# Attention tails of two heads in one product with both heads' values side by side, and one more batch's outputs turned by DMA

## The chip, the cores and the metric

The kernel runs on one core of one Trainium2 chip. The metric is the device time of one execution in microseconds (us). The kernel before was run eight times; one more execution was recorded by the hardware profiler, and all rows below come from that one.

The engines are TensorE (PE in the profile, its weight loads PEld), VectorE (DVE), ScalarE (ACT), GpSimd (POOL) and SyncE (SP). SyncE and GpSimd issue the DMAs; "SPq" and "POOLq" are their queues.

## The reference

Inputs are q, k and v of 8 batches x 8 heads x 576 positions x 64 elements, a forget gate f of 8 x 8 x 576, and two weight matrices of 512 x 2048 and 2048 x 512. A forgetting attention comes first, then a feed-forward layer with a gated activation:

```python
scores = scale * q @ k.T                     # per batch and head, 576 x 576
cum = np.cumsum(np.log(np.clip(f, 1e-4, 1)), axis=-1)
scores = where(causal, -1e9, scores + cum[:, None] - cum[None, :])
attn = softmax(scores)
x = (attn @ v)  ->  rows = batch x position (4608), columns = head x 64 (512)
h = x @ w_in
out = (h * sigmoid(h)) @ w_out               # 4608 x 512, float32
```

## The kernel before

**Attention.** The decay is folded into the values: each value row is multiplied by exp(-cum) of its position (up to a constant), and a 65th column holds that factor itself, so that one product gives both the weighted sum and the divisor. The unnormalised weights are exp(scores), kept in bf16 with keys on the partitions.

The 576 positions of a batch are split in three: the first 128 ("heads", done for all batches ahead of the loop), the next 384 ("rest", three blocks of 128), and the last 64 ("tail"). The main loop works on units n = 0 to 31. A unit is one batch b = n // 4 and two heads; two units make a query pair m = n // 2, so m = 0 to 15 and a batch is two pairs. For a unit:

- SyncE loads q and k of both heads (`load_qk`, L158), once a batch the tails (L168) and the values (L179). GpSimd casts to bf16 (`cast_qk`, L400 and L404) and scales the values by their weights (L414). SyncE turns q and k by a DMA transpose into `qkT` (`transposes`, L428).
- `scores` (L460) multiplies keys and queries in three chunks on TensorE; ScalarE takes the exponent into `u` (L464) for the rest rows and into `ut` (L476) for the tail rows; VectorE masks the diagonal blocks (L469, L483).
- `attend` (L491) multiplies the weights by the values into a PSUM tile `dn`: 18 matmuls of 65 columns for the six rest blocks (L507: two heads x three blocks), and ten for the tails (L516). VectorE takes the reciprocal of the 65th columns (L524) and multiplies (L525) into the SBUF tile `xr`.
- `back` (L532) turns a pair's `xr` so that model columns lie on the partitions, as the feed-forward part needs them. Where `BY_DMA[m]` is true this is two DMA transposes on SyncE's queue (L539 for the rest, L543 for the tails); else seven transposes on TensorE into a PSUM tile `tx` (L549) and two VectorE copies (L552, L555).

**The tail product before.** `ut` of a unit holds, for each of five key blocks, 64 weight columns of head 0, 64 columns of zeros, and 64 columns of head 1. The five matmuls of head 0 take the first 128 columns (head 0 and zeros) against head 0's values; the five of head 1 take the last 128 (zeros and head 1) against head 1's values, and all ten add into the same 128 x 65 block, so that head 0's 64 rows land on partitions 0 to 63 and head 1's on 64 to 127. The zeros are written once by GpSimd (L735).

**Feed-forward.** `m1_chunk` computes 128 of the 2048 inner columns of one group of rows: four matmuls into a PSUM tile `hp` (L568), a tanh on ScalarE (L576), and a multiply on VectorE into `gt` (L577). `m2_part` adds four matmuls of 512 columns each into a PSUM tile `po` (L613); after four parts ScalarE copies it out (L623) and GpSimd issues the store (L592).

**Order.** The order on every engine is that of the program text. In the loop over m, attention steps alternate with slots: `slot(us)` adds feed-forward steps worth so many microseconds by a fixed count of columns, from the groups of rows that are in `ready`. A batch's rest group gets into `ready` one slot after its second pair's `back`, or two slots after it where that pair goes by DMA. One iteration reads: scores of unit n, slot, `back(m - 1)`, the remaining scores of n and the first of n + 1, slot, the remaining scores of n + 1, slot, `attend(n)`, `attend(n + 1)`, slot.

**PSUM.** Scores have two double-bank buffers of their own. `dn`, `tx`, `hp` and `po` share the pool `pbig` with the tag "big" and four buffers of one bank each; a new tile can be written when the last reader of the buffer's former tile is done.

The lines of the loop that set this order:

```python
        scores(n + 1, 1)
        scores(n + 1, 2)
        slot(piece, 2)
        attend(n)
        attend(n + 1)
        slot(min(3.5, max(0.8, behind() - LAG)) if m > 1 else 0.8, 1)
```

The functions that the change touches:

Of the kernel before, what the change touches and what calls it, by code (L numbers as in the profile page):

```python
# [9 lines left out]
ALU = mybir.AluOpType  # L10
FP32 = mybir.dt.float32
BF16 = mybir.dt.bfloat16
P = 128
# [5 lines left out]
def kernel(  # L19
# [10 lines left out]
    nc = tc.nc  # L30

    B, H, S, D = q.shape
# [6 lines left out]
    ST = S - SM  # L39
    NM = SM // P  # L40
    NR = NM - 1
# [4 lines left out]
    NQ = NU // 2  # L46
# [9 lines left out]
    const = ctx.enter_context(tc.tile_pool(name="const", bufs=1))  # L56
# [4 lines left out]
    recp = ctx.enter_context(tc.tile_pool(name="recp", bufs=2))  # L61
# [7 lines left out]
    pbig = ctx.enter_context(tc.tile_pool(name="pbig", bufs=4, space=bass.MemoryType.PSUM))  # L69
# [12 lines left out]
    kT0 = [const.tile([P, NP, P], BF16, name=f"kT0_{b}") for b in range(B)]  # L82
    v0 = [const.tile([P, H, D + 1], BF16, name=f"v0_{b}") for b in range(B)]
    vps = [const.tile([P, NM, H, D + 1], BF16, name=f"vp_{i}") for i in range(2)]
    uts = [const.tile([P, NM + 1, 3, ST], BF16, name=f"ut_{i}") for i in range(4)]
    vfs = [const.tile([P, H, D + 1], FP32, name=f"vf_{i}") for i in range(4)]


# [10 lines left out]
    def xg(g):  # L99
        if g not in xgs:  # L100
            tag, bufs = {4 * P: ("x4", 1), 2 * P: ("x2" if g < 3 else "xt", 2), RB: ("x3", 3)}[GW[g]]
            xgs[g] = xpool.tile([P, NCC, GW[g]], BF16, name=tag, tag=tag, bufs=bufs)
        return xgs[g]
# [45 lines left out]
    def head(p, i):  # L149
        return p // 2 * 4 + 2 * i + p % 2  # L150
# [69 lines left out]
    for i in range(2):  # L220
        for g in range(2):
            nc.vector.tensor_copy(
                out=sel[:, i, :].rearrange("p (u w r) -> p u w r", u=2, w=2)[:, g, :, :],
                in_=ident_bf[:, :].rearrange("p (r u i w) -> p u i w r", u=2, i=2, w=2)[
                    :, g, i, :, :
                ],
            )

    def keep_warm(n):
# [7 lines left out]
        out=f_sb[:, :], in0=f_sb[:, :], scalar1=1e-4, scalar2=1.0, op0=ALU.max, op1=ALU.min  # L237
# [207 lines left out]
    def scores(n, c):  # L445
        b, p = divmod(n, NP)
        if c == 0:
            us[n] = upool.tile([P, 2, UW], BF16, name="u", tag="u")
        u, ut = us[n], uts[n % 4]
        t = qkT[n]  # L450
        sc = psc.tile([P, 2, SM], FP32, name="sc", tag="sc")
        for kb, q0, q1, o in CHUNKS[c]:
            for i in range(2):
                r = slice(i * D, (i + 1) * D)
                if kb == 0:
                    kt = kT0[b][r, p, :]
                else:
                    k0 = RB if kb == NM else kb * P + RB
                    kt = t[r, k0 : k0 + P]
                nc.tensor.matmul(  # L460
                    sc[:, i, o : o + q1 - q0], lhsT=kt, rhs=t[r, q0:q1], start=True, stop=True
                )
        w = SM if c < 2 else T0
        nc.scalar.activation(  # L464
            out=u[:, :, c * SM : c * SM + w], in_=sc[:, :, 0:w], func=ACT.Exp, scale=scale
        )
        if c == 0:
            x = u[:, :, 0:RB].rearrange("p i (a t) -> p i a t", t=P)
            nc.vector.tensor_tensor(  # L469
                out=x,  # L470
                in0=x,
                in1=tri[:, None, None, :].to_broadcast([P, 2, NR, P]),
                op=ALU.mult,
            )
        if c == 2:
            nc.scalar.activation(  # L476
                out=ut[:, :, 0:3:2, :].rearrange("p k i t -> p i k t"),
                in_=sc[:, :, T0 : T0 + (NM + 1) * ST].rearrange("p i (k t) -> p i k t", t=ST),
                func=ACT.Exp,
                scale=scale,  # L480
            )
            x = ut[:, NM, 0:3:2, :]
            nc.vector.tensor_tensor(  # L483
                out=x, in0=x, in1=trit[:, None, :].to_broadcast([P, 2, ST]), op=ALU.mult
            )

    NGR = 2 * NR + 1

    BY_DMA = [2 * 2 <= m < NQ - 1 for m in range(NQ)]

    def attend(n):  # L491
        b, p = divmod(n, NP)
        if p % 2 == 0:
            xqs[n // 2] = xqp.tile([P, NGR, 2, D], BF16, name="xr", tag="xr", bufs=3)
        xq = xqs[n // 2]
        u, ut = us.pop(n), uts[n % 4]
        dn = pbig.tile([P, NGR, D + 1], FP32, name="dn", tag="big")

        def vals(kb, i):
            h = head(p, i)  # L500
            return v0[b][:, h, :] if kb == 0 else vbf[b][:, kb - 1, h, :]

        for i in range(2):
            for c in range(1, NM):
                for kb in range(c + 1):
                    o = AT[c, kb]
                    nc.tensor.matmul(  # L507
                        dn[:, i * NR + c - 1, :],
                        lhsT=u[:, i, o : o + P],
                        rhs=vals(kb, i),  # L510
                        start=(kb == 0),
                        stop=(kb == c),
                    )
        for i in range(2):
            for kb in range(NM + 1):
                nc.tensor.matmul(  # L516
                    dn[:, NGR - 1, :],
                    lhsT=ut[:, kb, i : i + 2, :].rearrange("p i t -> p (i t)"),
                    rhs=vals(kb, i),
                    start=(i == 0 and kb == 0),  # L520
                    stop=(i == 1 and kb == NM),
                )
        rec = recp.tile([P, NGR], FP32, name="rec", tag="rec")
        nc.vector.reciprocal(out=rec[:, :], in_=dn[:, :, D])  # L524
        nc.vector.tensor_tensor(  # L525
            out=xq[:, :, p % 2, :],
            in0=dn[:, :, 0:D],
            in1=rec[:, :, None].to_broadcast([P, NGR, D]),
            op=ALU.mult,
        )  # L530

    def back(m):  # L532
        b, c0 = m // 2, m % 2 * 2
        xq = xqs.pop(m)
        g, t0 = TAILS_OF[b]
        xr = xg(REST_OF[b])[:, c0 : c0 + 2, :]
        xt = xg(g)[:, c0 : c0 + 2, :].rearrange("p i t -> p (i t)")[:, t0 * P : (t0 + 1) * P]
        if BY_DMA[m]:
            nc.sync.dma_start_transpose(  # L539
                out=xr.rearrange("p i (a q) -> p (i a) q", q=P),  # L540
                in_=xq[:, 0 : 2 * NR, :, :].rearrange("p c w d -> p (c w d)"),
            )
            nc.sync.dma_start_transpose(  # L543
                out=xt[:, None, :], in_=xq[:, 2 * NR, :, :].rearrange("p w d -> p (w d)")
            )
            return
        tx = pbig.tile([P, NGR, P], BF16, name="tx", tag="big")
        for c in range(NGR):
            nc.tensor.transpose(  # L549
                tx[:, c, :], xq[:, c, :, :].rearrange("p w d -> p (w d)"), ident_bf[:, :]  # L550
            )
        nc.vector.tensor_copy(  # L552
            out=xr, in_=tx[:, 0 : 2 * NR, :].rearrange("p (i a) q -> p i (a q)", i=2)
        )
        nc.vector.tensor_copy(out=xt, in_=tx[:, 2 * NR, :])  # L555
# [115 lines left out]
    def behind():  # L671
        t = sum(4 * (GW[g] / 2.4 + 2.5) for g, _ in M1[at["m1"] :] if g in ready)
        t += sum(4 * (DM / 2.4 + 2.5) for g, _, _ in M2[at["m2"] :] if g in ready)
        return t / 1000
# [56 lines left out]
    ready.add(0)  # L731
    nc.gpsimd.memset(trit[0:ST, :], 0.0)
    make_upper_triangular(nc, trit[ST:P, :], val=1.0, diag=True)
    for t in uts:
        nc.gpsimd.memset(t[:, :, 1, :], 0.0)  # L735
    for t in vps:
        nc.gpsimd.memset(t[0:ST, NR, :, :], 0.0)
    load_w_out(0)
# [84 lines left out]
    def slot(us_, first=0):  # L823
        n = len(stores)
        fill(us_, first)
        store(n)
        for x in pending:
            x[0] -= 1
        while pending and pending[0][0] == 0:
            ready.update(pending.pop(0)[1])  # L830

    for m in range(NQ):
        n = 2 * m
        piece = 1.7 if m < 2 else 2.4
        scores(n, 0)
        scores(n, 1)
        prepare(n)
        slot(piece, 2)
        if m > 0:
            back(m - 1)  # L840
            if m % 2 == 0:
                b = m // 2 - 1
                pending.append([1 + BY_DMA[m - 1], [REST_OF[b]] + ([TAILS_OF[b][0]] if b == NM - 1 else [])])
        scores(n, 2)
        scores(n + 1, 0)
        prepare(n + 1)
# [3 lines that stand above are left out]
        slot(piece, 2)  # L850
        attend(n)
        attend(n + 1)
        slot(min(3.5, max(0.8, behind() - LAG)) if m > 1 else 0.8, 1)
    back(NQ - 1)
    ready.update([REST_OF[B - 1], TAILS_OF[B - 1][0]])
# [36 lines left out]
```

The softmax here doesn't subtract the row's maximum and nothing guards it: scores larger than these inputs give would overflow.

## Time and profile before

| | |
|---|---|
| time, median of 8 runs | 346.88 us (346.48 to 347.54) |
| profiled execution | 346.72 us, its span 344.9 us |
| TensorE busy | 334.5 us, 97% |
| ScalarE busy | 218.2 us, 63% |
| VectorE busy | 184.2 us, 53% |
| GpSimd busy | 130.0 us, 38% |
| granted TensorE clock | full speed throughout |

The span is what the engines' rows cover; 1.8 us of the execution lie outside it. A row of a timeline gives the start in us, the duration in us, the engine, the line, the operation, and how many were merged; a bracket at its end says how long the engine sat idle before it and what ended that. A group row gives the count, the busy time in us, the mean of one in ns, and the idle time before them. A wait row says who waited for whom: us in total, times, the longest. TensorE's matmuls are pipelined, so the duration of one (some 0.19 us at 65 columns) is longer than the spacing between two.

### The profile page before, as it was taken

Reading aid. Unit: us, or ns where it says so; the run is one execution under the profiler, and the core shown is the slowest. Engines: PE = TensorE matmul, PEld = TensorE weight load, DVE = VectorE, ACT = ScalarE, POOL = GpSimd, SP = SyncE. Lnnn points to the kernel's source line nnn. Section 1 sums busy time; section 2 is a strip of 40 time slices with the busy share of each in tenths; the row PEclk is TensorE's granted clock in tenths of the full one; section 3 lists DMA queues with packets and bytes.
Section 4 is the critical chain, followed back from the end, with each engine's and each line's share of the span. In section 5 each row is a group of like instructions: output and inputs, shape, how many; then the busy total and the mean of one; then the engine's idle time right before and its main releaser. Section 6 shows DMA issues by size and latency. Waiting matters only on the chain.

```text
span 344.9 us, 8892 instructions
## 1 busy us (share of the span) xinstructions
PE 334.5 (97%) x3567; PEld 199.1 (58%) x3567; DVE 184.2 (53%) x389; ACT 218.2 (63%) x401; POOL 130.0 (38%) x227
## 2 busy tenths in 40 slices
PE   7999999988998999999999999999999999999995
PEld 3654556656655556566565665656656565555664
DVE  4766645456567457367547653646645454535330
ACT  5866554786586866767759566595775934545341
POOL 8995234934527154155227128135420000010011
PEclk9999999999999999999999999999999999999999
DMA  8999999999688998798988899989932000010103
GB/s 157 201 185 219 196 166 151 240 210 187 165 187 186 199 196 170 173 200 178 162 205 159 163 171 218 158 181 193 155 86 55 34 32 30 32 53 29 42 37 87
DMA packets 141497, 50.44 MB, mean 146 GB/s; under 512 B 132368, under 2 KB 138768, under 8 KB 141456
## 3 DMA queue, kind: packets, MB, share of 16 engines
q1 hardware_dynamic: 131440, 32.70, 53.2%
q0 software_dynamic: 9856, 17.04, 20.9%
q8 instruction: 28, 0.46, 0.6%
q10 hardware_dynamic: 160, 0.13, 0.1%
q14 instruction: 13, 0.11, 0.1%
HBM read 36.85 MB, written 9.44 MB: 134 GB/s over the span
## 4 chain that ended last, share of the span: by engine, by line
PE 72%; DMA 14%; SPq 5%; POOL 4%; issue 2%; ACT 1%; DVE 1%; POOLq 0%
PE po L613 30%; PE hp L568 28%; PE sc L460 6%; PE dn L507 4%; DMA vf<-in_v_dram 4%; DMA w_out_bf<-in_moe_w_out_dram 3%; DMA qktf<-in_k_dram 3%; PE dn L516 2%; SPq L158 2%; SPq L428 2%; DMA qkb<-in_k_dram 1%; DMA qkT<-qkb 1%; SPq L168 1%; DMA kf<-in_k_dram 1%; POOL qkb L131 1%
## 5 line engine op out<-in xcount | busy, mean ns | idle before, releaser
L576 ACT ACTIVATE th<-hp 128x384 bf16<-128x384 f32 (+2 forms) x208 | 95.9, 476 | 90.3 <-PE hp L568 88.0
L577 DVE SCALAR_TENSOR_TENSOR gt<-th,hp 128x384 bf16<-128x384 bf16 (+2 forms) x208 | 105.9, 521 | 79.7 <-ACT th L576 76.3
L613 PE MATMUL po<-w_out_bf,gt 128*128 128x512 bf16 (+1 forms) x592 | 144.7, 374 | 0.0
L568 PE MATMUL hp<-x,w_in_bf 128*128 128x384 bf16 (+2 forms) x704 | 128.9, 321 | 0.2
L568 PEld LDWEIGHTS <-w_in_bf 128*128 128x128 bf16 x832 | 78.5, 98 | 55.2 <-issue 2.2
L613 PEld LDWEIGHTS <-gt 128*128 128x128 bf16 x592 | 54.6, 98 | 49.6 <-issue 2.1
L464 ACT ACTIVATE u<-sc 128x1024 bf16<-128x1024 f32 (+1 forms) x96 | 75.0, 821 | 12.3 <-PE sc L460 12.2
L592 POOL DMA_DIRECT2D out_dram<-osb x38 | 21.0, 554 | 131.5 <-ACT osb L623 89.2
L414 POOL TENSOR_TENSOR vp<-vf,w_bf 128x520 bf16<-128x520 f32 (+1 forms) x32 | 35.0, 1096 | 31.4 <-DMA vf<-in_v_dram 26.3
L469 DVE TENSOR_TENSOR u<-u,tri 128x768 bf16<-128x768 bf16 x32 | 22.7, 709 | 19.8 <-ACT u L464 19.8
L623 ACT ACTIVATE osb<-po 128x512 f32<-128x512 f32 (+1 forms) x37 | 22.0, 595 | 12.3 <-PE po L613 12.2
L483 DVE TENSOR_TENSOR ut<-ut,trit 128x128 bf16<-128x128 bf16 x32 | 10.9, 340 | 34.9 <-ACT ut L476 32.8
L400 POOL CAST qkb<-qf 128x384 bf16<-128x384 f32 x32 | 17.7, 552 | 31.4 <-DMA qf<-in_q_dram 27.9
L460 PE MATMUL sc<-qkT 64*128 64x128 bf16 (+1 forms) x640 | 26.5, 207 | 2.3 <-DMA qkT<-qkb 2.3
L460 PEld LDWEIGHTS <-qkT 64*128 64x128 bf16 x640 | 18.2, 94 | 13.4 <-issue 8.1
L476 ACT ACTIVATE ut<-sc 128x640 bf16<-128x640 f32 x32 | 23.3, 727 | 0.0
L507 PEld LDWEIGHTS <-u 128*128 128x128 bf16 x576 | 20.7, 98 | 3.7 <-issue 1.3
L507 PE MATMUL dn<-vp,u 128*128 128x65 bf16 x384 | 21.8, 193 | 0.0
L507 PE MATMUL dn<-v,u 128*128 128x65 bf16 x192 | 19.8, 193 | 1.1 <-DVE gt L577 1.1
L525 DVE TENSOR_TENSOR xr<-dn,rec 128x448 bf16<-128x448 f32 x32 | 20.0, 625 | 1.1
L400 POOL CAST qkb<-kf 128x384 bf16<-128x384 f32 x32 | 16.7, 522 | 7.5 <-DMA kf<-in_k_dram 7.5
L568 PE MATMUL hp<-xt,w_in_bf 128*128 128x256 bf16 x128 | 18.2, 272 | 0.3 <-DVE gt L577 0.2
(68 smaller groups left out, 203.6 us busy)
## 6 DMA issues: line engine op xcount, KB each, us to landing
out_dram<-osb POOLq DMA_DIRECT2D x32, 256.0 KB, 3.1
vf<-in_v_dram SPq DMA_DIRECT2D x26, 256.0 KB, 5.0
qf<-in_q_dram SPq DMA_DIRECT2D x64, 96.0 KB, 2.8
kf<-in_k_dram SPq DMA_DIRECT2D x64, 96.0 KB, 2.9
w_in_bf<-in_moe_w_in_dram POOLq DMA_DIRECT2D x4, 512.0 KB, 7.0
w_out_bf<-in_moe_w_out_dram POOLq DMA_DIRECT2D x4, 512.0 KB, 8.8
vf<-in_v_dram POOLq DMA_DIRECT2D x6, 256.0 KB, 10.2
qkb<-in_q_dram POOLq DMA_DIRECT2D x8, 128.0 KB, 5.1
```

What stands on the lines that cost most here:

```text
L400: nc.gpsimd.tensor_copy(out=t2[:, c0 : c0 + NR, :].rearrange("p c x -> p (c x)"), in_=t[:, :, :, :].rearrange("p c h d -> p (c h d)"),)
L414: nc.gpsimd.tensor_tensor(out=vbf[b][r, c, :, :], in0=vst[b][c][r, :, :], in1=w_bf[r, c + 1, b * H : (b + 1) * H, None].to_broadcast([n, H ...
L460: nc.tensor.matmul(sc[:, i, o : o + q1 - q0], lhsT=kt, rhs=t[r, q0:q1], start=True, stop=True)
L464: nc.scalar.activation(out=u[:, :, c * SM : c * SM + w], in_=sc[:, :, 0:w], func=ACT.Exp, scale=scale)
L469: nc.vector.tensor_tensor(out=x, in0=x, in1=tri[:, None, None, :].to_broadcast([P, 2, NR, P]), op=ALU.mult,)
L476: nc.scalar.activation(out=ut[:, :, 0:3:2, :].rearrange("p k i t -> p i k t"), in_=sc[:, :, T0 : T0 + (NM + 1) * ST].rearrange("p i (k t) ...
L507: nc.tensor.matmul(dn[:, i * NR + c - 1, :], lhsT=u[:, i, o : o + P], rhs=vals(kb, i), start=(kb == 0), stop=(kb == c),)
L568: nc.tensor.matmul(hp[:, :], lhsT=w_in_bf[:, cc, fc * P : (fc + 1) * P], rhs=xcols(g, cc), start=(cc == 0), stop=(cc == NCC - 1),)
L576: nc.scalar.activation(out=th[:, :], in_=hp[:, :], func=ACT.Tanh, scale=0.5)
L577: nc.vector.scalar_tensor_tensor(out=gt[:, fc, :], in0=th[:, :], scalar=1.0, in1=hp[:, :], op0=ALU.add, op1=ALU.mult,)
L613: nc.tensor.matmul(po[:, :], lhsT=gt[:, fc, tb * P : (tb + 1) * P], rhs=w_out_bf[:, fc, m0:m1], start=(fc == 0), stop=(fc == NFC - 1),)
L623: nc.scalar.activation(out=osb[:, :], in_=po[:, :], func=ACT.Copy, scale=0.5)
```

## The change

The tails leave `attend`, which keeps only the six rest blocks. A new function `attend_tails(m)` runs after both units of a pair: for each unit, five matmuls multiply the 128 weight columns of both heads by the values of both heads side by side (130 columns). The result holds four blocks of 64 x 65, of which two are used: head 0's rows with head 0's values, and head 1's rows with head 1's. VectorE takes one reciprocal for both units and then multiplies once for partitions 0 to 63 and once for 64 to 127. The zero columns of `ut` and the GpSimd writes of them go. `BY_DMA` becomes true for m = 2 and 3 too, so that batch 1's outputs are turned by DMA and its rest group gets ready one slot later.

```diff
-    uts = [const.tile([P, NM + 1, 3, ST], BF16, name=f"ut_{i}") for i in range(4)]
+    uts = [const.tile([P, NM + 1, 2, ST], BF16, name=f"ut_{i}") for i in range(4)]
...
-    BY_DMA = [2 * 2 <= m < NQ - 1 for m in range(NQ)]
+    BY_DMA = [2 <= m < NQ - 1 for m in range(NQ)]
...
-        dn = pbig.tile([P, NGR, D + 1], FP32, name="dn", tag="big")
+        dn = pbig.tile([P, 2 * NR, D + 1], FP32, name="dn", tag="big")
...
-        for i in range(2):
-            for kb in range(NM + 1):
-                nc.tensor.matmul(
-                    dn[:, NGR - 1, :],
-                    lhsT=ut[:, kb, i : i + 2, :].rearrange("p i t -> p (i t)"),
-                    rhs=vals(kb, i),
-                    start=(i == 0 and kb == 0),
-                    stop=(i == 1 and kb == NM),
-                )
...
+    def attend_tails(m):
+        b, h0 = m // 2, m % 2 * 4
+        xq = xqs[m]
+        dt = pbig.tile([P, 2, 2, D + 1], FP32, name="dt", tag="big")
+        for w in range(2):
+            ut = uts[(2 * m + w) % 4]
+            for kb in range(NM + 1):
+                vals = v0[b] if kb == 0 else vbf[b][:, kb - 1, :, :]
+                nc.tensor.matmul(
+                    dt[:, w, :, :],
+                    lhsT=ut[:, kb, :, :].rearrange("p i t -> p (i t)"),
+                    rhs=vals[:, h0 + w : h0 + 4 : 2, :],
+                    start=(kb == 0),
+                    stop=(kb == NM),
+                )
+        rec = recp.tile([P, 2, 2], FP32, name="rect", tag="rect")
+        nc.vector.reciprocal(out=rec[:, :, :], in_=dt[:, :, :, D])
+        for i in range(2):
+            r = slice(i * ST, (i + 1) * ST)
+            nc.vector.tensor_tensor(
+                out=xq[r, 2 * NR, :, :],
+                in0=dt[r, :, i, 0:D],
+                in1=rec[r, :, i, None].to_broadcast([ST, 2, D]),
+                op=ALU.mult,
+            )
...
-    for t in uts:
-        nc.gpsimd.memset(t[:, :, 1, :], 0.0)
...
         attend(n)
         attend(n + 1)
+        attend_tails(m)
```

More of the change, by code (lines that the diff above doesn't have):

```diff
@@ L476, in scores @@
             nc.scalar.activation(
-                out=ut[:, :, 0:3:2, :].rearrange("p k i t -> p i k t"),
+                out=ut[:, :, :, :].rearrange("p k i t -> p i k t"),
                 in_=sc[:, :, T0 : T0 + (NM + 1) * ST].rearrange("p i (k t) -> p i k t", t=ST),
@@ L481, in scores @@
             )
-            x = ut[:, NM, 0:3:2, :]
+            x = ut[:, NM, :, :]
             nc.vector.tensor_tensor(
@@ L495, in attend @@
         xq = xqs[n // 2]
-        u, ut = us.pop(n), uts[n % 4]
-        dn = pbig.tile([P, NGR, D + 1], FP32, name="dn", tag="big")
+        u = us.pop(n)
+        dn = pbig.tile([P, 2 * NR, D + 1], FP32, name="dn", tag="big")
         def vals(kb, i):
@@ L513, in attend @@
                     )
-        for i in range(2):
-            for kb in range(NM + 1):
-                nc.tensor.matmul(
-                    dn[:, NGR - 1, :],
-                    lhsT=ut[:, kb, i : i + 2, :].rearrange("p i t -> p (i t)"),
-                    rhs=vals(kb, i),
-                    start=(i == 0 and kb == 0),
-                    stop=(i == 1 and kb == NM),
-                )
-        rec = recp.tile([P, NGR], FP32, name="rec", tag="rec")
+        rec = recp.tile([P, 2 * NR], FP32, name="rec", tag="rec")
         nc.vector.reciprocal(out=rec[:, :], in_=dn[:, :, D])
         nc.vector.tensor_tensor(
-            out=xq[:, :, p % 2, :],
+            out=xq[:, 0 : 2 * NR, p % 2, :],
             in0=dn[:, :, 0:D],
-            in1=rec[:, :, None].to_broadcast([P, NGR, D]),
+            in1=rec[:, :, None].to_broadcast([P, 2 * NR, D]),
             op=ALU.mult,
         )
+    def attend_tails(m):
[23 more added lines that the diff above has]
+            )
     def back(m):
```

## The prediction

> **What bounds the kernel now.** I read the busy times first, then TensorE's waits, the chain of waits where it is broken, and at last VectorE's and SyncE's own rows.
>
> ```profile
> PE 334.5 (97%) x3567; PEld 199.1 (58%) x3567; DVE 184.2 (53%) x389; ACT 218.2 (63%) x401; POOL 130.0 (38%) x227
> ```
>
> TensorE sets the time; VectorE is busy half of it. The waits of TensorE between 60 and 280 us (attention beside the feed-forward part), in us, times, longest:
>
> ```profile
> PE sc L460 <- DMA qkT<-qkb: 2.3, 2, 1.5
> PE dn L507 <- DVE gt L577: 1.1, 1, 1.1
> PE hp L568 <- DVE gt L577: 0.2, 1, 0.2
> ```
>
> The two waits for qkT end at 74.31 and 85.89 us, the third at 107.96. What TensorE saves before a wait whose end something else sets only lengthens that wait. The chain around the third (start, us, what):
>
> ```profile
> 100.22 0.39 PE tx L549 x7
> ...
> 105.75 1.69 DVE ut L483
> 107.44 0.47 DVE gt L577
> 107.96 0.70 PE dn L507 x18
> 108.66 0.30 PE dn L516 x10
> 108.96 0.55 PE dn L507 x18
> ```
>
> One mask (L483, median 0.23 us) takes 1.69 us while GpSimd casts and scales values without a break from 105.14 to 108.5 us. GpSimd follows the loads, so I take this stall as fixed in time. After 107.96 TensorE has no gap over 0.24 us until the tail: there every column saved counts, and every new wait.
>
> VectorE at one pair's end (query pair 5; start, us), and TensorE's next work after the products:
>
> ```profile
> 134.28 1.21 DVE L577 SCALAR_TENSOR_TENSOR gt<-th,hp 128x384 bf16<-128x384 bf16 x2 [0.19 <-ACT th L576]
> 135.40 0.20 DVE L524 RECIPROCAL rec<-dn 128x7 f32<-128x7 f32 x1
> 135.63 0.63 DVE L525 TENSOR_TENSOR xr<-dn,rec 128x448 bf16<-128x448 f32 x1
> 136.17 0.20 DVE L524 RECIPROCAL rec<-dn 128x7 f32<-128x7 f32 x1
> ```
> ```profile
> 135.91 2.12 PE L568 MATMUL hp<-x,w_in_bf 128*128 128x384 bf16 x12
> ```
>
> **The tail products.** Ten matmuls of 65 columns take 0.30 us (the chain's row), 30.4 ns each; 18 take 0.55, the same. So weight loads (98 ns each in their own row) are hidden and columns pay: 65 columns at the 0.4165 ns each of a 512-column matmul (216 less about 3 ns) are 27 ns, plus 3. The new product has 130 columns: 54 + 3 = 57 ns; the seven 128-column transposes above (0.39 us, 56 ns each) are the nearest row and agree. A pair of units had 20 x 30.4 = 0.61 us and gets 10 x 57 = 0.57: 0.04 saved. Sixteen pairs give 0.64; the 13 whose products run from 107.96 on give 0.5.
>
> [...]
>
> **Second batch by DMA.** For m = 2 and 3 the seven transposes (0.39 us on TensorE) and two VectorE copies (0.55 + 0.21 us) go. The first 0.39 lies before 107.96 and is lost in the stall there; the second counts. Saved on the path: 0.5 + 0.39 = 0.9 us.
>
> The order of work changes in one place: batch 1's rest becomes ready one slot later, so pair 4 does eight more output-projection matmuls before its attends and more first-projection chunks after. The total is the same: nothing, as long as the transposed x has landed. x(3) is issued near 116.6 to 117.8 us (the place of 116.12, delayed as below) and lands 3.1 us later (median), 119.7 to 120.9; its first reader stands at about 121.5. If that cover is gone, the price is what the landing is late.
>
> **Zero rows no longer written.** Four GpSimd memsets (1.28 us together from 21.71) stand ahead of the w_out load on whose landing the query loads wait. DMA is at 1.1 to 1.25 mean share from 16 to 36 us, and a value load issued at 19.15 lands only at 29.3, so that queue is backed up and an earlier issue moves nothing: 0 taken, bounds 0 and 1.28 gained.
>
> **VectorE and the four buffers.** A pair had 2 x (0.203 + 0.625) = 1.66 us of division. The rows by shape:
>
> ```profile
> L525 DVE TENSOR_TENSOR xr<-dn,rec 128x448 bf16<-128x448 f32 x32 | 20.0, 625 | 1.1
> L375 DVE TENSOR_TENSOR xq<-dn,rec 128x512 bf16<-128x512 f32 x5 | 3.5, 692 | 0.2
> L375 DVE TENSOR_TENSOR xq<-dn,rec 128x256 bf16<-128x256 f32 x6 | 2.5, 423 | 0.2
> L374 DVE RECIPROCAL rec<-dn 128x4 f32<-128x4 f32 x4 | 0.7, 176 | 0.0
> ```
>
> 512 against 256 elements gives 1.05 ns an element plus 154: 384 take 0.557, 128 take 0.288. New: 2 x (0.20 + 0.557) + 0.176 + 2 x 0.288 = 2.27 us, 0.6 more a pair. As VectorE is half idle, that alone is hidden. What isn't is the order of buffers. Of four "big" PSUM buffers one mostly holds an unfinished output sum, so three rotate. In the built program of before, dn, dn and the next hp take three, and only the second hp reuses the first dn; of after, dn, dn, dt take them, and in 15 of 16 pairs the very first hp takes the first dn's buffer (in pair 10 a free one). Its weight load then waits for L525's successor; behind it in TensorE's queue stands everything.
>
> Timing from the first dn matmul, t0: before, the buffer was needed at t0 + 1.71 + 0.65 = 2.36. Now at 2 x 0.55 + 0.57 = 1.67. The buffer is free 0.23 + 0.557 = 0.79 us after the reciprocal begins, plus 0.04 for the signal (107.44 + 0.47 to 107.96). Where VectorE is idle, the reciprocal begins 0.19 us after the last matmul of dn (147.12 + 0.86 to 148.17), now t0 + 0.74: free at 1.57, no wait, 0.1 left. That holds for pairs 4, 6, 7, 8, 9, 12, 13, 15. Where hp chunks stand just before, VectorE is still at their gt: in pair 5 (t0 = 134.20) the reciprocal can't begin before 1.20, free at 2.03: 0.36 late, and some 0.08 more for the second dn and dt behind it: 0.44. By the same reading pair 14 (reciprocal at 263.24, t0 = 262.04) 0.36, pair 11 (219.97, t0 = 218.92) 0.22, pair 3 0.02. Pair 2's 0.4 and those of pairs 0 and 1 vanish in the stalls that follow them. New waits on the path: 1.04; bounds 0.5 (reads of 384 end sooner, no second wait) and 1.8 (0.1 more in each of eight pairs with no margin).
>
> **SyncE.** Each moved batch half puts two more transposes into its queue:
>
> ```profile
> 106.36 1.22 SPq L428 DMA_TRANSPOSE qkT<-qkb  x1
> 109.95 2.41 SPq L428 DMA_TRANSPOSE qkT<-qkb  x1
> ...
> 129.02 1.21 SPq L539 DMA_TRANSPOSE x<-xr  x1
> 130.28 1.23 SPq L543 DMA_TRANSPOSE xt<-xr  x1
> ```
>
> From 102 to 245 us SyncE is issuing with hardly a gap. x(2) and xt(2) enter ahead of qkT(9) at 106.36, x(3) and xt(3) ahead of qkT(11) at 116.12: 2 x 2.55 = 5.1 us. A gap of 0.8 before 106.36 takes some, the stretched 2.41 (usually 1.22) perhaps 1.2 more: later loads and transposes come 3.1 to 4.3 us late. The leads over their readers: qkT(9) 3.5 us (delay there 1.8), qkT(13) 6.3, x(5) 5.4 (issued 140.67, landing 3.1 later, read at 149.2). All hold, the last by 1.1: 0 taken.
>
> **Sum.** -0.9 + 1.04 = +0.1 on the profiled 344.9 us span; with 1.8 us outside it 346.72 becomes 346.85, and as the runs' median is 0.16 above that run, 347.0. Own bounds: -0.4 to +0.9, 346.5 to 347.8.
>
> **Rivals.** *The stall at 108 goes and the cover holds*: with no 0.76 us of copies in pair 3, VectorE meets GpSimd elsewhere; 1.1 us returns, or the GpSimd shift gives up to 1.28. Against: L483 starts when ScalarE lets it, and GpSimd doesn't move. Gain 0.9 to 2.0: 344.9 to 346.0. *SyncE's queue decides, slower*: if the added transposes also lengthen landings (x took 2.4 to 4.7) and stretch qkT issues as at 109.95, x(5) comes 4.3 + 1.4 + 1.2 = 6.9 us later against a lead of 5.4: 1.5 us of wait; from 5.4 us on it decides. 347.9 to 348.6. *Weight loads did cost*: at 98 ns for each of the 160 that go, 15.7 us, 331; the 30.4 ns spacing speaks against it.
>
> **How the numbers follow.** Forecast 0.44, first rival 0.26, SyncE 0.27, weight loads 0.03. About 0.2% (0.7 us) is what a measurement can tell from no change. Faster: most of the first rival, the last, a little of the forecast, 0.3; slower: SyncE's and the upper edge of the forecast, 0.34; the same 0.36. The likeliest alone is 346.5 to 347.8; 345.3 to 348.7 leaves out 2 in 10.
>
> **What would show it.** Right: dt matmuls at 57 ns; the tail divisions near 0.29 us; hp after dt waiting for VectorE's division some 0.4 us in pairs 5 and 14 and not in 6 and 8; the wait at 108 us still there. Wrong: no waits of hp for the division; waits of hp for x or sc for qkT past 108 us; dt well under 57 ns.

## The result and the profile after

The kernel after takes 350.57 us (median of 20 runs, 347.86 to 353.40), the one before in the same comparison 347.33 us (57 runs). The ratio is 1.0083, with a 95% interval of 1.0063 to 1.0103: slower by more than 0.2%, and outside the predicted 345.3 to 348.7. The profiled execution of after took 351.89 us with a span of 350.1, against 346.72 and 344.9 before. In all comparisons here, runs far above the fastest of their kernel are left out of the ratio, though not of the medians.

The engines' busy times of after (busy us, share, instructions), and TensorE's waits between 60 and 290 us (in total, times, longest):

```profile
PE 338.0 (97%) x3393; PEld 197.8 (56%) x3393; DVE 191.2 (55%) x433; ACT 218.1 (62%) x401; POOL 128.7 (37%) x223
```
```profile
PE hp L587 <- DMA x<-xr: 2.0, 1, 2.0
PE sc L460 <- DMA qkT<-qkb: 1.8, 2, 1.0
PE dn L507 <- DVE gt L596: 1.2, 1, 1.2
```

The last two lines are those of before (2.3 and 1.1). The first is new: once, the feed-forward part waits for x(3), batch 1's turned outputs. TensorE has 174 instructions fewer and yet 3.5 us more of busy time. The chain of waits shows where the wait and about half of that busy time sit (start, us, what), and TensorE's timeline gives the rows around it:

```profile
117.94 2.61 PE po L632 x12
120.55 3.99 DMA x<-xr
124.54 0.04 issue
124.59 4.76 PE hp L587 x18
```
```profile
122.15 0.49 PE L587 MATMUL hp<-x,w_in_bf 128*128 128x384 bf16 x2
124.59 4.76 PE L587 MATMUL hp<-x,w_in_bf 128*128 128x384 bf16 x18 [1.95 <-DMA x<-xr]
```

TensorE had finished at 122.64 and stood for 1.95 us. Then 18 matmuls of 384 columns took 4.76 us, where a kernel below does the same 18 in 3.11. The table of stretches says why. A row gives the stretch, its length, the busy time of PE, PEld, DVE, ACT and POOL, and then the granted TensorE clock, the DMA share and GB/s:

```profile
125.00:126.00 1.00, 1.00 (x6) 0.52 (x5) 0.37 (x1) 0.49 (x1) 0.00 (x0) 0.62 0.87 162
126.00:127.00 1.00, 1.00 (x5) 0.45 (x4) 0.56 (x2) 0.49 (x1) 0.00 (x0) 0.50 0.75 171
127.00:128.00 1.00, 1.00 (x5) 0.44 (x3) 0.28 (x2) 0.49 (x1) 0.00 (x0) 0.50 0.78 178
128.00:129.00 1.00, 1.00 (x5) 0.49 (x4) 0.46 (x1) 0.34 (x1) 0.00 (x0) 0.68 0.67 145
```

The clock is at half speed, with TensorE fully busy. Adding up what is missing to 1.00, 0.38 + 0.50 + 0.50 + 0.32, gives 1.70 us of work lost. So this wait costs twice: 1.95 us of standing, and nearly as much behind it.

**The account.** The first `dn` matmul of pair 3 and that of pair 15 bound the part in which the prediction said that everything counts: 107.96 and 276.05 us before (168.09), 108.89 and 281.02 after (172.13). After lost 4.04 us there; 0.93 us was lost ahead of pair 3, a point that lies anywhere from 107.6 to 109.7 us in the profiles of the kernels here (112.45 in the last one below); what moves it was not tried. Pair by pair: from pair 4 to 5, +3.32; from 5 to 6, +0.45; from 11 to 12, +0.10; from 14 to 15, +0.34; the eight others sum to -0.17, with -0.03 to -0.05 in five of them and nothing in three. The +3.32 is 1.95 of wait and 1.65 of clock, less the 0.39 of transposes that went; 0.1 stays unassigned.

**All runs, not only the profiled one.** Each run comes with its mean granted clock. Half a clock for 3.4 of 350 us is 0.005, so a run with one such fall shows 0.995, as the profiled execution does. Counting one execution more than the median above does (353.20 us), after has 10 runs at 0.998 to 1.000, median 349.06 us, ten at 0.994 or 0.995, median 351.97, and one at 0.990. The mean does not say where the clock fell, and before shows the dip too (21 of its 66 runs beside the experiments, median 348.08, against 346.93 in the 43 without it; two far-off runs, 354.39 and 1196.34, are left aside); waits for qkT near 75 us are a candidate there (1.45 us kept the clock in the profile of before, 2.35 lost it in that of the second batch alone). But the dip is dearer in after, 2.9 us against 1.2. Which executions lose the clock is not settled. In the profiles here waits of up to 1.73 us kept it, and the 1.95 us of after lost it (last section): the wait for x(3) may be shorter in the executions that keep it, or something else may decide. One profile of after can't tell these apart.

### The profile page after: what moved, and what is told of

Same layout as the page of the kernel before. It is cut to its first block, busy times and chain, and to the rows that moved or that the text cites. A ratio compares the mean times of both kernels' runs of the same rounds, so it can differ in the third digit from the quotient of the medians.

```text
span 350.1 us, 8609 instructions
## 1 busy us (share of the span) xinstructions
PE 338.0 (97%) x3393; PEld 197.8 (56%) x3393; DVE 191.2 (55%) x433; ACT 218.1 (62%) x401; POOL 128.7 (37%) x223
## 4 chain that ended last, share of the span: by engine, by line
PE 69%; DMA 14%; POOL 5%; SPq 4%; issue 3%; ACT 2%; DVE 2%; POOLq 0%
PE po L632 29%; PE hp L587 27%; PE sc L460 6%; PE dn L507 4%; DMA w_out_bf<-in_moe_w_out_dram 4%; DMA vf<-in_v_dram 3%; SPq L158 3%; DMA qktf<-in_k_dram 2%; PE dt L533 2%; DMA kf<-in_k_dram 2%; DMA qkb<-in_k_dram 1%; DMA x<-xr 1%; DMA qkT<-qkb 1%; POOL v L341 1%; SPq L168 1%
## 5 line engine op out<-in xcount | busy, mean ns | idle before, releaser
L587 PE MATMUL hp<-x,w_in_bf 128*128 128x384 bf16 (+2 forms) x704 | 130.6, 324 | 2.3 <-DMA x<-xr 2.0
L483 DVE TENSOR_TENSOR ut<-ut,trit 128x128 bf16<-128x128 bf16 x32 | 12.7, 396 | 36.0 <-ACT ut L476 36.0
L469 DVE TENSOR_TENSOR u<-u,tri 128x768 bf16<-128x768 bf16 x32 | 21.1, 659 | 16.7 <-ACT u L464 16.7
L507 PEld LDWEIGHTS <-u 128*128 128x128 bf16 x576 | 19.9, 97 | 4.4 <-issue 1.8
L507 PE MATMUL dn<-v,u 128*128 128x65 bf16 x192 | 18.9, 193 | 1.4 <-DVE gt L596 1.2
L507 PE MATMUL dn<-vp,u 128*128 128x65 bf16 x384 | 20.2, 193 | 0.0
L516 DVE TENSOR_TENSOR xr<-dn,rec 128x384 bf16<-128x384 f32 x32 | 17.8, 558 | 1.1
```

Of the source, the lines that this page charges most:

```text
L469: nc.vector.tensor_tensor(out=x, in0=x, in1=tri[:, None, None, :].to_broadcast([P, 2, NR, P]), op=ALU.mult,)
L507: nc.tensor.matmul(dn[:, i * NR + c - 1, :], lhsT=u[:, i, o : o + P], rhs=vals(kb, i), start=(kb == 0), stop=(kb == c),)
L587: nc.tensor.matmul(hp[:, :], lhsT=w_in_bf[:, cc, fc * P : (fc + 1) * P], rhs=xcols(g, cc), start=(cc == 0), stop=(cc == NCC - 1),)
```

## The experiments

The theory to test (A in the expectations): the second batch's x(3) lands late, because SyncE issues it late, and the clock is lost behind the wait. Its rivals: the tails' product costs by its order of buffers; or neither does, and the loss is the shift ahead of pair 3.

**1. The tails' product alone, and the second batch alone.** Before decides `BY_DMA` by `2 * 2 <= m`, after by `2 <= m`. The first kernel is after with the former, the second is before with the latter.

```diff
-    BY_DMA = [2 <= m < NQ - 1 for m in range(NQ)]
+    BY_DMA = [2 * 2 <= m < NQ - 1 for m in range(NQ)]
```

> The tails' part alone: batch 1's outputs are turned on TensorE again. Theory A (the first projection of batch 1's rest waits for x(3), and the granted clock falls after that wait): the wait at 124.6 us is gone and so is the halved clock behind it; what is left is waits for the division of 0.2 to 0.4 us in pairs 5, 11 and 14 less 0.5 us of columns: between -0.3 and +0.6 us against before. Theory B (the division that holds the first dn's buffer is the loss): +2 to +3 us, as in the whole change.

Measured: 348.07 us against 347.29, ratio 1.0021 (1.0001 to 1.0041). No wait for x, clock 1.00 in the profile, and 168.73 us from pair 3 to pair 15: 0.64 more than before, in pairs 5 (+0.44), 11 (+0.10) and 14 (+0.34), less 0.03 to 0.04 in most others.

> The other part alone: the tails as before, batch 1's outputs by DMA. Theory A: the wait for x of some 2 us and the half clock of some 3.5 us after it appear here as well; +2 to +3.5 us against before. Theory B: nothing of the loss; 0.4 to 0.8 us faster than before, from the transposes that TensorE no longer does.

Measured: a median of 351.38 us in two groups, four runs from 346.37 to 347.48 and eight from 349.43 to 354.15; ratio 1.0043 (1.0003 to 1.0082). The profile is of an execution of the upper group, 353.07 us; the bracket gives the idle time before the row:

```profile
126.42 4.76 PE L568 MATMUL hp<-x,w_in_bf 128*128 128x384 bf16 x18 [2.75 <-DMA x<-xr]
```

The same wait and the same slow 18 matmuls, with the old tails. So the second batch by DMA brings the wait by itself, and the lower group, at before's own time and a mean clock of 0.997 to 0.999, fits executions that miss it (seven of the upper eight are at 0.985 to 0.995). Theory A holds for the larger part, the tails' product costs some 0.7 us (0.03 to 1.4 by the interval), and the shift ahead of pair 3 explains neither.

**2. Move the reader, or move the issue.** Two mends: batch 1's rest gets ready one slot later, or in pair 4 `back(m - 1)`, which issues x(3), goes ahead of `prepare(n)`, which issues the next loads of q and k.

```diff
-                pending.append([1 + BY_DMA[m - 1], [REST_OF[b]] + ...
+                pending.append([1 + BY_DMA[m - 1] + (m == 4), [REST_OF[b]] + ...
```

> The whole change, but batch 1's rest group becomes ready one slot later still (pair 5's first slot instead of pair 4's last), so its first reader stands some 2 to 4 us later. Theory A: no wait for x, clock at full speed throughout; between -0.5 and +0.6 us against before. Theory B or a queue of SyncE's that is simply too full: the loss stays, +2 to +3 us.

Measured: 353.05 us, ratio 1.0152 (1.0124 to 1.018), 2.5 us slower than the change. The wait for x(3) went, and another came:

```profile
150.06 1.14 PE L587 MATMUL hp<-x,w_in_bf 128*128 128x384 bf16 x6 [1.55 <-DMA x<-xr]
```

That is x(5), the victim that the prediction's rival named. So theory A's expectation for this kernel failed: the loss stayed, though not at x(3). The slots fill themselves by a count of columns, so what isn't drawn in one slot is replaced by other work, and the first reader of batch 2's rest met its transfer in flight. TensorE also waited 2.5 us in `dn` for `gt`, 1.7 of them in the stall near 108 us. Moving a reader in such an order moves the readers behind it.

```diff
+        if m == 4:
+            back(m - 1)
         prepare(n)
```

> The whole change, but in pair 4 the two DMA transposes of pair 3's outputs enter SyncE's queue ahead of that pair's qkT transpose and loads, some 5 us earlier; SyncE then waits for pair 3's division with the loads behind it. The sum of SyncE's work is the same. Theory A: x lands before its reader, no wait, full clock: between -0.6 and +0.6 us against before. If the fullness of SyncE's queue is the loss (the queue's total work, whatever its order): +2 us or more, with waits of the scores for qkT.

Measured: 348.69 us, ratio 1.0041 (1.0016 to 1.0066): 1.9 us less than the change, though 1.4 over before, where theory A allowed 0.6. x(3) is issued at 113.84 us and no wait for x is left. The chain of waits, where after had the transfer:

```profile
121.60 0.57 PE dt L533 x10
122.18 3.29 PE hp L587 x20
```

Twenty matmuls in 3.29 us: full clock. So the place of x(3) in SyncE's queue did decide. The median is 0.6 us over that of the tails alone, which the two intervals don't tell apart; from pair 3 to pair 15 the profile takes 168.80 us, the tails alone 168.73. Two of the ten runs (352.71 and 353.64) are at a mean clock of 0.990, and no profile shows why.

**3. Take the divisions' wait away.** The tails' product after the pair's last slot, so that `hp` no longer follows it (batch 1's outputs by TensorE, as before):

```diff
-        attend_tails(m)
         slot(min(3.5, max(0.8, behind() - LAG)) if m > 1 else 0.8, 1)
+        attend_tails(m)
```

> As e1_tails_only (batch 1 on TensorE), but the pair's tail products stand after the slot that follows the attends, so that dn, dn, and two or more hp or po come before dt takes a buffer. If the division that holds the first dn's buffer is what e1_tails_only lost, the 1.4 us of weight-load waits for it (and 0.8 us for the tails' division) vanish, and the columns saved show: 0.4 to 0.8 us faster than before, about 1.2 us faster than e1_tails_only. If the tail product itself costs more than its columns say, it stays 0.5 to 1 us slower than before.

Measured: 348.89 us, ratio 1.0039 (1.0012 to 1.0066): no gain over the tails alone. From pair 3 to pair 15 it takes 168.31 us, only 0.22 over before, but at the end the last pair's transposes meet the division that was put off:

```profile
284.86 0.23 PE L568 MATMUL tx<-ident_bf,xr 128*128 128x128 bf16 x1 [0.98 <-DVE xr L544]
```

The second attempt, also with batch 1's outputs by TensorE, leaves the tails in place and gives `dt` one of the scores' double banks instead of a "big" one:

```diff
-        dt = pbig.tile([P, 2, 2, D + 1], FP32, name="dt", tag="big")
+        sc = psc.tile([P, 2, SM], FP32, name="sc", tag="sc")
+        dt = sc[:, :, 0 : 2 * (D + 1)].rearrange("p w (i e) -> p w i e", i=2)
```

> As e1_tails_only, but dt takes a scores' double bank in place of a big buffer, so that after the products the first hp finds a free bank and only the second takes the first dn's, as in the kernel before. If the waits for the division come from the buffers' order, they vanish (no weight load of an hp waits for xr), and the 0.04 us a pair of columns show: 0.2 to 0.7 us faster than before and 0.7 to 1.3 us faster than e1_tails_only. If they come from VectorE's 0.6 us more a pair as such, this is as slow as e1_tails_only, 0.5 to 0.9 us slower than before.

Measured: 348.15 us, ratio 1.0035 (1.0011 to 1.0059). From pair 3 to 15 it takes 168.46 us; pair 5's +0.44 fell to +0.09 and pair 14's +0.34 to +0.23, but now the scores wait for the division in pair 3, and did once at 71 us:

```profile
112.15 0.34 PE L460 MATMUL sc<-qkT,kT 64*128 64x384 bf16 x2 [0.23 <-DVE xr L545]
```

That the order of buffers causes the wait is shown by pair 5; a net gain is not. In both, the wait turned into another.

**4. Keep the clock up through the wait.** Twelve matmuls of zeros go into the first `hp` of batch 1's rest ahead of its own, so that TensorE works where it stood. Their result is overwritten.

```diff
+        if g == REST_OF[1] and fc == 0:
+            for _ in range(12):
+                nc.tensor.matmul(hp[:, :], lhsT=warm[:, 0:P], rhs=warm[:, 0:w], start=True, stop=True)
```

> The whole change, with twelve matmuls of zeros (384 columns each, 12 x 0.163 = 1.96 us) written into the first hp tile of batch 1's rest ahead of its own products, where TensorE waits for x. The tile is overwritten by the real products. If only the wait for x costs time, this is no faster than the change: the same or up to 2 us slower (where x was in time). If the fall of the granted clock after the wait costs some 1.7 us of its own, the clock stays full, and this is 1 to 2 us faster than the change in spite of 2 us more work, 1 to 2 us slower than before.

Measured: 350.89 us, ratio 1.0106 (1.0071 to 1.014), no faster than the change. The profile shows the filler doing its part:

```profile
122.51 2.11 PE L588 MATMUL hp<-warm 128*128 128x384 bf16 x12
...
125.93 3.11 PE L590 MATMUL hp<-x,w_in_bf 128*128 128x384 bf16 x18 [0.99 <-DMA x<-xr]
```

The same 18 matmuls in 3.11 us instead of 4.76, after a wait of 0.99, and all six runs are at 0.997 to 1.000. So the 1.65 us were the clock's. But where an execution keeps its clock anyway, the filler is new work: 349.06, the median of after's such runs, plus 1.94 us of filler (122.51 to 124.45) is 351.0, and 350.89 came out. That reading fits; it isn't shown by itself. The expectation had reckoned from the profiled execution as if every execution were like it.

**5. Both mends, and half of the second batch.** Experiment 2's early issue with experiment 3's deferral:

```diff
+        if m == 4:
+            back(m - 1)
...
+        attend_tails(m)
```

> e4_x3_first with the tail products after the slot. Theory A and the buffer term together: no wait for x, no wait for the division; 0.5 to 1.3 us faster than before, if the pair-3 stall near 108 us stays as it was. If the longer queue of SyncE costs by other waits (qkT, values), 0 to 1.5 us slower than before.

Measured: 352.45 us, ratio 1.0113 (1.0069 to 1.0157), its six runs from 348.70 to 357.41. In the profile x(5) is late, by 2.30 us at 152.25, the clock is 0.88 in the stretch from 144 to 158, and the last pair's 0.98 is there again. As in experiment 2, once x(3) is safe the next transfer with little lead comes up.

```diff
-    BY_DMA = [2 <= m < NQ - 1 for m in range(NQ)]
+    BY_DMA = [m == 2 or 2 * 2 <= m < NQ - 1 for m in range(NQ)]
```

> As e5_tails_deferred, but pair 2's outputs by DMA (x(2) has over 10 us until its reader) and pair 3's on TensorE; batch 1's rest becomes ready as before. Takes 0.39 us from TensorE and puts 2.55 us into SyncE's queue ahead of qkT(9), whose lead was 3.5 us. If nothing else waits: 0 to 0.4 us faster than e5_tails_deferred. If the stall near 108 us fixes everything ahead of it: the same as e5_tails_deferred.

Measured, with the deferral: 349.70 us, ratio 1.0051 (1.003 to 1.0073). Only x(2) is added to SyncE's queue, and still a wait for x of 1.22 us appears, at 179.44. Its median is 0.8 us over that of the deferral alone, though the two intervals overlap.

**6. Does SyncE's issue time matter, or what is in flight?** GpSimd issues the value loads of batches 2 and 3, whose issue kept SyncE 4.27 us for one batch in the trace of before (at 97.66).

```diff
-        nc.sync.dma_start(
+        (nc.gpsimd if b in (2, 3) else nc.sync).dma_start(
```

> The whole change, but the value loads of batches 2 and 3 (four DMAs each, 4.2 us of SyncE's issue time a batch) are issued by GpSimd. [...] If x(3) is late because SyncE's queue issues it late, it is now issued some 3 to 4 us earlier against pair 3's products, lands before its reader, and the wait and the half clock are gone: 0 to 1 us slower than before, 2 to 3 us faster than the change. If it is late because the DMA engines are full, the wait stays: 2 to 3 us slower than before.

Measured: 356.68 us against 346.82, ratio 1.0286 (1.0235 to 1.0336). That is far beyond both branches of the expectation. SyncE's timeline, GpSimd's, and the chain of waits:

```profile
119.14 1.28 SPq L558 DMA_TRANSPOSE x<-xr  x1
```
```profile
117.70 3.41 POOL L179 DMA_DIRECT2D vf<-in_v_dram  x4
```
```profile
119.14 10.05 DMA x<-xr
```

x(3) was issued 1.4 us earlier than in after, and landed 4.7 us later: 10.05 us in flight instead of 3.99, with the value loads issued beside it. TensorE waited 6.60 us. SyncE's issue time alone is thus not the limit. As the loads' issuer is all that differs from after, what else is in flight is the likely reason for the longer landing.

The same together with the scores' buffer of experiment 3:

> e10_values_by_gpsimd and e11_tails_score_buffer together: both parts of the change, the x landing in time and the buffers' order restored. If both causes are the right ones and the only ones, 0.4 to 1.2 us faster than before; if SyncE's queue still delays a later x or qkT, 0.5 to 3 us slower with such a wait in the profile.

Measured: 356.49 us, ratio 1.0255 (1.0203 to 1.0307). The wait for x is 3.5 us and one for qkT 2.1, and the mean clock of its six runs is 0.978 to 0.995. So the loads' cost dominates, and the buffer adds nothing to be seen. No variant beat the kernel before.

## Why the prediction was wrong

**The step that failed** is the sentence on batch 1's rest: "nothing, as long as the transposed x has landed". It named the cover and the price if the cover fails, and then sized the cover wrongly. Put on the clock of the first `dn` of pair 3, x(3)'s place in SyncE's queue was +8.16 before (116.12) and its issue +11.66 after (120.55): 3.5 us later, where 0.5 to 1.7 was allowed. SyncE's rows show the pieces:

```profile
102.94 2.64 SPq L428 DMA_TRANSPOSE qkT<-qkb  x1
...
108.13 1.21 SPq L558 DMA_TRANSPOSE x<-xr  x1
109.44 1.18 SPq L562 DMA_TRANSPOSE xt<-xr  x1
...
114.31 2.49 SPq L428 DMA_TRANSPOSE qkT<-qkb  x1
...
120.55 1.34 SPq L558 DMA_TRANSPOSE x<-xr  x1
```

The pair x(2), xt(2) took 2.59 us and the gap gave back 0.8, as foreseen. But the qkT at 102.94 stretched to 2.64 from 1.28, and the stretched one (2.41 before) was not absorbed, it came again as 2.49. Some 0.3 more came from single rows such as a load of q and k at 1.26 instead of 1.02. Then the landing: 3.99 us, not the median of 3.1, though 2.4 to 4.7 stood in the prediction's own text as a rival's condition. The trace of before had it already: the two `x` transposes nearest in time, at 129.02 and 140.67, landed after 4.2 and 4.7 us, and the median is of all eleven. With these, the prediction's latest issue would have landed at 122.0 to 122.5, behind the reader; and the lead of x(5), put at 5.4 us with the median, was 3.8. The prediction's latest landing, 120.9, left 0.6 us before its reader at 121.5. In the trace of after (all 0.93 us later) the reader was ready at 122.64, some 0.2 later still. 1.8 us of issue and 0.9 of landing, less a cover of 0.8, make 1.9; 1.95 was measured.

**The missing term** is the clock. The prediction priced a late landing at "what the landing is late". In the profiled execution it was that plus 1.65 us.

**The rival "SyncE's queue decides"** had the mechanism (longer issues, longer landings) and the wrong first victim. x(5) held in the change and x(3) failed; x(5) did fail, by 1.55 and 2.30 us, in two of the three kernels where x(3) was mended. Its price of 1.5 us was for one wait at full clock.

**What held.** In pair 7, where nothing waits, ten dt matmuls stand between 167.38 and the hp at 167.96: 58 ns each, predicted 57, and five of the eight pairs without a named wait gain 0.03 to 0.05, predicted 0.04. The rival of weight loads that cost failed: each of these matmuls has its own load (3393 of each in after), and 174 TensorE instructions fewer brought no gain near its 15.7 us. The divisions, by shape (min/median/max in ns), predicted 557 and 288:

```profile
L516 DVE TENSOR_TENSOR xr<-dn,rec x32: 557/558/559, 69.0 to 282.7; 128x384 bf16<-128x384 f32 x32
L544 DVE TENSOR_TENSOR xr<-dt,rect x32: 282/289/295, 70.4 to 283.7; 64x128 bf16<-64x128 f32 x32
```

The waits for buffers are in the pairs named and nearly of the size named: 0.44 predicted in pair 5 and 0.49 found (the 0.45 of the account and the 0.04 that the columns give back), 0.36 and 0.38 in pair 14, 0.22 and 0.14 in pair 11, and none over 0.05 in the others after pair 4. VectorE and TensorE in pair 5:

```profile
139.66 0.19 DVE L515 RECIPROCAL rec<-dn 128x6 f32<-128x6 f32 x1
139.88 0.56 DVE L516 TENSOR_TENSOR xr<-dn,rec 128x384 bf16<-128x384 f32 x1
```
```profile
138.46 0.19 PE L507 MATMUL dn<-v,u 128*128 128x65 bf16 x1
...
139.79 0.22 PE L533 MATMUL dt<-v,ut 128*128 128x130 bf16 x1
...
140.50 2.23 PE L587 MATMUL hp<-x,w_in_bf 128*128 128x384 bf16 x12
```

`hp` starts 0.06 us after the first division's end at 140.44, and 2.04 us after the first `dn`; in pair 7 it is 1.67 us, from 166.29 to 167.96. The prediction had 2.03 and 1.67. With the tails alone the terms of the sum, -0.5 and +1.04, make +0.54 from pair 3 to 15, and 0.64 was measured: 1.00 of waits in the three pairs named, and -0.36 for the rest. The stall at 108 us stayed (1.17 us). That the earlier GpSimd writes gain nothing was not tried by itself.

## What to carry to other kernels

Cover is a difference of two times, so give each its own range: wherever the queue runs without a gap, take the worst issue and the worst landing in the trace or those nearest in time, not the median of the whole. Price a wait of TensorE at its length plus what the clock may lose behind it (1.95 and 1.65 us in the profile of after), and look at the run's mean clock to see in how many executions that happens. Where work is drawn by a fixed count, a mend that moves one reader moves the next transfer into its place, so check the lead of the second-shortest transfer before moving the first.

## What the runs showed of the hardware

**The clock fell in or behind waits of 1.95 us and more.** From 60 to 270 us, these idle times of TensorE, among others, kept 1.00: 1.22 us at 179 us (half of the second batch), 1.45 at 74 (before), 1.55 at 150 and 1.73 at 108 (batch 1's rest later). In or behind these it fell, with the granted clock as the mean of stretches of 14 us; no other stretch from 60 to 270 us of these profiles is below 1.00:

| kernel | TensorE idle | until | granted clock |
|---|---|---|---|
| after | 1.95 us | 124.59 us | 0.88 from 116 to 130 |
| values by GpSimd with the scores' buffer | 2.08 | 104.76 | 0.88 from 102 to 116 |
| early issue with deferral | 2.30 | 152.25 | 0.88 from 144 to 158 |
| second batch alone | 2.35 | 76.12 | 0.88 from 74 to 88 |
| second batch alone | 2.75 | 126.42 | 0.92 from 116 to 130, 0.96 from 130 to 144 |
| values by GpSimd with the scores' buffer | 3.55 | 130.49 | 0.97 from 116 to 130, 0.79 from 130 to 144 |
| values by GpSimd | 6.60 | 129.24 | 0.83 from 116 to 130, 0.93 from 130 to 144 |

In after the fall came not in the wait but 0.65 us behind it: if the clock is at 0.50 where it isn't full, 0.62 in the stretch from 125 means from 125.24, and 0.68 in that from 128 means until 128.64, 3.40 us in all. In the second batch alone the second fall begins, by the same working, at 127.66, 1.24 us behind the wait:

```profile
127.00:128.00 1.00, 1.00 (x7) 0.55 (x6) 0.53 (x1) 0.84 (x2) 0.00 (x0) 0.83 0.76 172
```

A fall can also lie ahead of 60 us: in the kernel with half of the second batch the page shows a granted clock of 8 tenths in the slice from 17.4 to 26.2 us, and that run's mean is 0.995. What decides between the 1.73 us that kept the clock and the 1.95 that lost it is not shown; each stands in one profile.

**Transposes took longer beside loads from another queue.** An x transpose that lands in 3.99 us took 10.05 with four value loads issued by GpSimd from 1.4 us ahead of it, and a qkT issue on SyncE at 94.72 in that kernel, just behind four such loads at 90.35, took 4.90 us, where its other qkT issues from 89 to 131 us took 1.22 to 1.52. Other transfers were in flight too, so that the loads did it is likely, not shown alone.
